# A new hand-written order, wider weights in one small product, and a last scaling on two engines in a banded-attention and mixture-of-experts kernel

## The chip, the cores and the metric

One Trainium2 chip; the kernel runs on one of its cores. The metric is the device time of one execution in microseconds (us). Times inside an execution come from one profiled execution and count from the start of its span.

## The reference

Attention over a band of 65 tokens (batch 8, 8 heads, 576 tokens, head size 64) is followed by a layer in which each of the 4608 tokens goes to the one expert with the largest biased logit. The bias depends on the token's modality, which is 0 or 1.

```python
mask = np.abs(pos[:, None] - pos[None, :]) <= 32
scores = np.where(mask, (q @ k^T) / 8, -1e9); attn = softmax(scores); x = attn @ v      # x: [4608, 512]
logits = x @ w_gate + modality_bias[modality_id]                                        # 8 experts
e_idx = argmax(logits); gate_w = softmax(logits)[e_idx]
out[mask_e] = gate_w * (relu(x[mask_e] @ w1[e]) @ w2[e])                               # w1: 512x1024, w2: 1024x512
```

The kernel assumes that the bias decides, so that all tokens of a modality go to one expert. It checks this on the chip by flags and has a general path behind a branch, which is not taken with the inputs drawn.

## The kernel before

The program is one straight list of steps. A string, `ORDER`, names the steps, and a loop at its end calls them one after another; each engine then executes its own instructions in that order and waits only on semaphores. Nothing reorders them later. A step such as `U1.2:7` has a name (`U`), numbers (token tile 1, part 2) and the PSUM banks it writes (7); a suffix such as `/a`, `/v`, `/p` picks ScalarE (ACT), VectorE (DVE) or GpSimd (POOL). A step in front of another on the same engine therefore delays it, whatever it waits for.

Attention, per batch element b (8 of them): `l` loads a half of q or k (GpSimd's DMA queue, 288 KB, into a ring of 8 buffers), `lw` and `lv` load v; `t` and `tv` transpose on DVE; `TV` and `vc` finish v for b = 0, 1, 2. `SA`/`SB` are the score products, with `MA`/`MB` adding a band mask for the first three halves; `sa`/`sb` are the exponentials on ACT. `M` multiplies by a 0/1 mask on DVE where `MA`/`MB` were not used; that mask is built by `Ka` and spread by `Kb`, both on POOL. `V` is the product with v, `v` divides by the row sum on DVE.

Sorting by modality: `Kh` clears a buffer (DVE), `Ki` loads the modality ids into it (five DMAs on SP's queue), `Kd`, `Kt0` to `Kt2` and `Kr0` to `Kr2` turn them into places by counting (`lpf`, `offs`). `o` makes a one-hot matrix from `lpf` (five compares on POOL, or one on DVE). `H` multiplies x by it, `a` copies the sorted columns into `xl`; `J` multiplies four numbers per token (`valx`) by it and `j` copies those into `cl`. Modality 0 fills `xl` from the left, modality 1 from the right; tiles 0 to 17 (256 tokens, even numbers from the left) and the extra tile 18 (128 tokens, in the middle, with weights of its own) are made of it.

Experts: `W1.i` and `W2.i` load the weights of modality i (2: the extra tile), each 1 MB in bf16, on GpSimd's queue; the expert's number is read from `sp_i`. `G` and `r` make logits, gate and row number of a tile pair; `U` is the first product (8 matmuls of 256 columns, four parts a tile), `u` the relu, `D` the second product in halves (4 matmuls of 512 columns), `y` scales by the gate weight, and `O` scatters 128 rows to the output by an indirect DMA from POOL. `X` is a pair of matmuls on zeros that fill an otherwise idle TensorE. `N` is a drain of POOL. `Kc6`, `Kf0` and `Kf2` prepare limits and flags on POOL; `Z` steps end in the flag that the last branch reads.

GpSimd's DMAs rotate over eight semaphores; one of them is issued only when the DMA eight before it has landed. PSUM has eight banks, `xl` is shared by all tiles, the results of `y` rotate over six buffers.

Of the kernel before, what the change touches and what calls it, by code (L numbers as in the profile page):

```python
# [43 lines left out]
J0:45 j0.0 j0.1 j0.2 j0.3 j0.4 v3 t1.1.0 tv1.0 MA1.0:0123 X13:6 SA1.0:0123 tv2.0 tv1.1 t2.0.0 t2.0.1 sa1.0 SB1.1:4567
X1:3 TV1.0:012 X8:3 sb1.1 vc1.0/a SA1.1:4567 H0.0:3 H0.1:0 V4:12 sa1.1 TV1.1:567 H0.3:4 v4 H0.2:1 X12:2 H0.4:2 Kb/p
lw2.1 W1.1 l2.1.1 l2.0.1 o2/p a0.0 a0.1 a0.2 a0.3 a0.4 W1.0 M7 vc1.1/v V5:01 l3.0.0 Kg l3.1.0 J1:34 W2.1 l3.1.1 Ky1
V7:56 v5 j1.0 j1.1 j1.2 j1.3 j1.4 l3.0.1 v7 TV2.0:012 U1.2:7 SA2.0:3456 M6 vc2.0/a U1.3:0 V6:12 sa2.0 u1.3/a SB2.0:3456
sb2.0 u1.2/v W2.0 l4.1.0 U1.0:0 tv2.1 v6 H1.0:1 u1.0/a a1.0 t2.1.0 t2.1.1 M9 H1.1:2 U1.1:7 u1.1/v M8 TV2.1:345 H1.2:0
U0.3:6 U0.2:1 u0.3/v vc2.1/a a1.1 a1.2 u0.2/a V9:34 H1.4:2 H1.3:5 G0:0 V8:67 a1.3 a1.4 v9 U0.1:1 SB2.1:2345 r0.5 v8 G1:6
r0.0 r1.0 r0.1 r1.1 t3.0.1 r0.2 u0.1/a sb2.1 U0.0:0 U2.2:1 u0.0/v SA2.1:2345 U2.0:7 U2.3:0 u2.2/a sa2.1 r1.5 r1.2 t3.0.0  # L50
E1 u2.3/a SA3.0:1234 Kc8 lv3.0 l4.0.0 D1.0.0:5 U2.1:0 sa3.0 SB3.0:1234 u2.0/a u2.1/a M11 t3.1.1 r0.7 M10 E0 r0.3 r0.4
t3.1.0 sb3.0 D1.1.0:6 D1.0.1:5 U3.2:0 y1.0/v Ko1 V10:12 D1.1.1:6 V11:34 y1.1/a U3.0:5 U3.3:6 u3.3/a u3.2/v v10 v11
SA3.1:0123 u3.0/v J2:45 sa3.1 j2.0 j2.1 j2.2 D2.0.0:7 U3.1:6 SB3.1:0123 D2.0.1:7 M12 r1.7 r1.3 t4.0.1 r1.4 y2.0/v M13
j2.3 u3.1/a j2.4 D0.1.0:6 H2.1:5 H2.2:4 H2.0:7 D0.1.1:6 sb3.1 V13:12 D2.1.0:0 y0.1/v t4.0.0 v13 H2.3:3 a2.0 a2.1 a2.2
D2.1.1:0 y2.1/a a2.3 M15 SB4.0:4567 V12:12 D0.0.0:0 H2.4:3 sb4.0 D0.0.1:0 v12 M14 lv3.1 V15:12 y0.0/v v15 l4.1.1 r0.6
t4.1.1 SA4.0:4567 l4.0.1 O1.1 a2.4 U4.2:3 u4.2/a U4.0:0 u4.0/a sa4.0 r1.6 l5.1.0 lv4.0 O1.0 o3/p l5.0.0 t4.1.0 U4.3:1
U5.3:0 V14:23 SB4.1:4567 u5.3/v sb4.1 v14 U4.1:0 G2:2 U5.2:3 u5.2/a SA4.1:4567 sa4.1 u4.1/a l5.1.1 lv4.1 u4.3/v r2.5
r2.0 t5.0.1 D3.1.0:1 U5.0:2 H3.1:3 H3.0:5 u5.0/a D3.1.1:1 H3.4:0 H3.2:2 H3.3:4 J3:67 a3.0 a3.1 j3.0 a3.2 D3.0.0:5 M17
y3.1/v M16 t5.0.0 U5.1:1 j3.1 a3.3 V17:23 D3.0.1:5 a3.4 j3.2 y3.0/a j3.3 U7.2:4 u7.2/a j3.4 U7.3:0 u7.3/a u5.1/a r2.1
M18 v17 V16:23 SA5.0:4567 U7.0:0 U7.1:1 l5.0.1 M19 Kc6 O0.1 O2.0 Z1 l6.1.0 o4/p O0.0 v16 t5.1.1 r2.2 V19:23 sa5.0 v19  # L60
SB5.0:4567 u7.1/a u7.0/a sb5.0 D4.0.0:1 D4.1.0:0 V18:23 t5.1.0 E2 v18 SB5.1:4567 D4.0.1:1 G3:2 D5.1.0:3 sb5.1 SA5.1:4567
r2.3 o5/v r2.4 r3.5 r3.0 r3.1 l6.0.0 O3.1 r2.6 O2.1 sa5.1 D4.1.1:0 H4.0:2 D5.1.1:3 a4.0 J4:45 r3.2 r3.7 t6.0.1 y4.0/v E3
j4.0 lv5.0 lv5.1 j4.1 t6.0.0 D7.0.0:1 H4.4:2 D7.0.1:1 H4.2:6 D5.0.0:7 r3.3 r3.4 y5.1/v j4.2 j4.3 j4.4 y4.1/a H4.1:0 a4.1
a4.2 H4.3:3 a4.3 D5.0.1:7 a4.4 U6.1:0 M23 M21 M20 r2.7 M22 y7.0/a y5.0/a V21:45 v21 u6.1/v U6.0:6 V20:23 v20 U8.1:1
D7.1.0:0 SB6.0:2345 sb6.0 u6.0/v u8.1/v D7.1.1:0 V23:67 U9.0:1 G4:5 U8.0:2 V22:34 l6.0.1 v23 o6/v r4.0 t6.1.0 v22 O4.0
o7/p r3.6 l6.1.1 O3.0 O7.0 l7.0.1 O4.1 l7.0.0 l7.1.1 lv6.1 O5.1 U8.2:6 U9.3:7 u9.3/v t6.1.1 u9.0/a u8.0/a y7.1/a
SA6.0:0123 U8.3:4 u8.2/a sa6.0 u8.3/v U9.2:6 SA6.1:0123 H5.0:4 r4.1 t7.1.0 r4.5 u9.2/a U6.2:7 U9.1:6 u9.1/v sa6.1
SB6.1:0123 U6.3:5 t7.0.0 u6.3/v u6.2/a a5.0 H5.2:7 D6.1.0:4 D8.0.0:6 sb6.1 H5.1:0 J5:12 D8.0.1:6 D6.1.1:4 a5.1 a5.2
D6.0.0:0 H5.3:5 D9.0.0:3 D6.0.1:0 H5.4:7 D9.0.1:3 lv6.0 Kf0 M26 r4.2 r4.7 t7.1.1 E4 j5.0 j5.1 j5.2 j5.3 y6.1/a j5.4 a5.3
r4.3 M25 r4.4 M27 V26:12 y8.0/v M24 a5.4 y9.0/a D8.1.0:4 v26 y6.0/a V27:56 SB7.1:0123 v27 U10.2:7 D8.1.1:4 V24:56  # L70
u10.2/v O7.1 l7.1.0 r4.6 O5.0 lv7.0 O9.0 lv7.1 Kf2 O8.0 O6.0 O6.1 U11.3:7 v24 u11.3/v t7.0.1 sb7.1 y8.1/a SA7.1:0123
U11.0:5 U10.0:4 V25:67 sa7.1 SB7.0:0123 u10.0/v v25 u11.0/v sb7.0 U10.1:4 G5:6 U10.3:5 SA7.0:0123 M31 r5.0 u10.1/v sa7.0
U11.2:7 D10.1.0:4 H6.0:0 U11.1:3 u10.3/v r5.1 r5.2 r5.5 a6.0 E5 r5.3 r5.4 H6.2:1 J6:56 H6.4:0 H6.1:2 u11.1/a D11.1.0:3
# [5 lines left out]
D12.1.1:4 D12.0.1:3 Kf3:1 r6.4 r6.7 G7:5 Kf4 U14.1:6 U16.0:7 U17.2:1 u14.1/v u17.2/a U15.2:6 u15.2/a y12.1/v y13.0/v
U15.3:0 G9:6 G8:1 r7.0 r7.5 r8.5 y13.1/a U17.3:2 r7.6 r6.6 r8.6 U15.1:5 r7.1 r8.0 y12.0/v r7.2 r7.7 U14.2:4 U14.0:1  # L80
u14.0/a U17.0:3 u17.0/a U14.3:1 E7 u15.1/a u17.3/a u14.3/a u14.2/a D14.1.0:3 D14.0.0:5 U17.1:1 U15.0:4 D14.0.1:5 r7.3
r8.1 r7.4 r8.2 r8.7 O13.1 O12.0 O12.1 r9.0 r9.1 r9.2 W1.2 U16.1:2 u17.1/a D17.0.0:1 D14.1.1:3 y14.0/a u15.0/a u16.0/a E9
Z0 r9.5 y14.1/a E8 r9.3 r8.3 r8.4 r9.7 r9.4 u16.1/v U16.3:4 D15.0.0:5 D15.1.0:3 D17.1.0:6 D16.0.0:2 D17.1.1:6 O13.0 W2.2
# [1002 lines left out]
```

## Time and profile before

| | us |
|---|---|
| three runs | 226.16, 227.04, 223.16 (median 226.16) |
| profiled execution | 223.96 |
| its span | 222.3 |
| busy: TensorE | 204.5 (92%) |
| busy: DVE | 154.7 (70%) |
| busy: ACT | 141.0 (63%) |
| busy: POOL | 118.7 (53%) |

The profile lists each engine's busy time, how long it waited and which engine or DMA ended each wait. A row of its timeline gives start, duration, engine, line of the code, operation, output and input, the number of instructions in the row, and in brackets the idle time before it with what ended it. PE is TensorE's matmuls, PEld its weight loads, SPq the sync engine's DMA issues, and a q behind an engine its sequencer. In the windows view each engine has its busy time and, in brackets, its number of instructions in the stretch; PEclk is the clock that TensorE was granted, 1.00 being full speed, and the DMA share is that of 16 DMA engines.

### The profile page before, as it was taken

Reading aid. Unit: us, or ns where it says so; the run is one execution under the profiler, and the core shown is the slowest. Engines: PE = TensorE matmul, PEld = TensorE weight load, DVE = VectorE, ACT = ScalarE, POOL = GpSimd, SP = SyncE. Lnnn points to the kernel's source line nnn. Section 1 sums busy time; section 2 is a strip of 40 time slices with the busy share of each in tenths; the row PEclk is TensorE's granted clock in tenths of the full one; section 3 lists DMA queues with packets and bytes.
Section 4 is the critical chain, followed back from the end, with each engine's and each line's share of the span. In section 5 each row is a group of like instructions: output and inputs, shape, how many; then the busy total and the mean of one; then the engine's idle time right before and its main releaser. Section 6 shows DMA issues by size and latency. Waiting matters only on the chain.

```text
span 222.3 us, 6507 instructions
## 1 busy us (share of the span) xinstructions
PE 204.5 (92%) x2669; PEld 145.6 (66%) x2696; DVE 154.7 (70%) x302; ACT 141.0 (63%) x234; POOL 118.7 (53%) x215
## 2 busy tenths in 40 slices
PE   6759888999999999999999999999999999999960
PEld 2436657789666678786577875787488659765620
...
GB/s 68 197 201 131 123 155 207 223 200 212 212 186 205 165 160 196 104 122 138 10 42 154 180 187 193 51 196 4 0 3 143 94 50 3 167 194 204 188 157 55
DMA packets 34055, 30.44 MB, mean 137 GB/s; under 512 B 24889, under 2 KB 24929, under 8 KB 33633
## 3 DMA queue, kind: packets, MB, share of 16 engines
...
q8 instruction: 23, 0.38, 0.7%
q14 instruction: 16, 0.12, 0.2%
q1 hardware_dynamic: 224, 0.05, 0.1%
HBM read 40.96 MB, written 9.70 MB: 228 GB/s over the span
## 4 chain that ended last, share of the span: by engine, by line
PE 76%; DMA 9%; POOL 6%; issue 2%; DVE 2%; SPq 1%; POOLq 0%; DVEq 0%
PE banks L845 28%; PE banks L822 28%; DMA w_sb<-in_moe_w_dram 6%; PE banks L660 6%; PE banks L614 5%; POOL oh L573 3%; PE banks L680 3%; DMA mid<-in_moe_modality_id_dram 2%; PE banks L749 2%; PE banks L711 1%; DVE cl L415 1%; POOL out_dram L866 1%; SPq L285 1%; PE banks L252 1%; POOL qkin L217 1%
## 5 line engine op out<-in xcount | busy, mean ns | idle before, releaser
L866 POOL DMA_INDIRECT out_dram<-ys,ix x37 | 38.9, 1051 | 70.4 <-issue 27.9
L822 PE MATMUL banks<-xl,w_sb 128*128 128x256 bf16 x576 | 70.7, 273 | 0.7 <-DMA w_sb<-in_moe_w_dram 0.7
L845 PE MATMUL banks<-w_sb,hT 128*128 128x512 bf16 x267 | 67.7, 379 | 1.1
L822 PEld LDWEIGHTS <-w_sb 128*128 128x128 bf16 x576 | 53.8, 98 | 11.0 <-issue 1.1
L622 ACT ACTIVATE pt<-banks 128x1536 bf16<-128x1536 f32 x32 | 46.3, 1449 | 18.6 <-PE banks L614 18.4
L837 ACT ACTIVATE hT<-banks 128x512 bf16<-128x512 f32 x45 | 25.8, 599 | 30.0 <-PE banks L822 29.8
L845 PEld LDWEIGHTS <-hT 128*128 128x128 bf16 x296 | 26.6, 98 | 25.5 <-issue 0.5
L582 DVE STREAM_TRANSPOSE qk<-qkin 128x576 int32<-128x576 int32 x32 | 39.0, 1243 | 1.2 <-DMA qkin<-in_q_dram 0.6
L698 ACT CAST xl<-banks 128x704 f32 (+1 forms) x40 | 28.4, 710 | 8.7 <-PE banks L680 8.2
L641 DVE TENSOR_TENSOR pt<-pt,mask 128x1920 bf16<-128x1920 bf16 x26 | 29.8, 1160 | 0.5 <-ACT pt L626 0.3
L671 DVE TENSOR_TENSOR xt<-banks,recs 128x640 bf16<-128x640 f32 x32 | 26.4, 825 | 1.2
L835 DVE TENSOR_SCALAR hT<-banks 128x512 bf16<-128x512 f32 x29 | 19.6, 682 | 9.0 <-PE banks L822 7.9
L660 PEld LDWEIGHTS <-pt 128*128 128x128 bf16 x576 | 21.1, 97 | 2.8 <-DVE pt L641 0.2
L660 PE MATMUL banks<-vt,pt 128*128 128x65 bf16 x576 | 22.6, 193 | 0.0
L573 POOL TENSOR_SCALAR oh<-io_l,lpf 128x128 bf16<-128x128 bf16 x30 | 19.9, 682 | 2.7 <-PE banks L680 1.9
L858 ACT ACTIVATE ys<-banks,gw 128x512 f32<-128x512 f32 x19 | 12.8, 685 | 12.4 <-PE banks L845 9.1
L860 DVE TENSOR_SCALAR ys<-banks,gw 128x512 f32<-128x512 f32 x18 | 13.2, 743 | 10.6 <-PE banks L845 10.5
L614 PE MATMUL banks<-qk 32*128 32x192 bf16 (+1 forms) x640 | 18.9, 240 | 1.4 <-DVE qk L582 1.3
L614 PEld LDWEIGHTS <-qk 32*128 32x128 bf16 x640 | 12.5, 93 | 8.3 <-issue 6.9
L217 POOL DMA_DIRECT2D qkin<-in_k_dram x16 | 10.3, 642 | 12.1 <-DMA w_sb<-in_moe_w_dram 7.8
L680 PEld LDWEIGHTS <-xt 128*128 128x128 bf16 x160 | 11.2, 114 | 4.6 <-issue 0.7
...
## 6 DMA issues: line engine op xcount, KB each, us to landing
...
pt<-in_moe_w_dram POOLq DMA_DIRECT2D x2, 1024.0 KB, 10.3
...
out_dram<-ys,ix POOLq DMA_INDIRECT x37, 4.0
mid<-in_moe_modality_id_dram SPq DMA_DIRECT2D x3, 8.0 KB
```

The costliest lines, as they stand in the source:

```text
L573: gp.tensor_scalar(out=t_[:, m, :], in0=io_l[:], scalar1=lpf[:, NM * b + m:NM * b + m + 1], scalar2=None, op0=ALU.is_equal)
L582: nc.vector.transpose(qk_t[b % 2][:, g, at:at + S].rearrange("p (t r) -> p r t", r=R), Ct["l", b, u, g][:].bitcast(I32).rearrange("p (r j) ...
L614: nc.tensor.matmul(st[:, h, WIN * i_:WIN * i_ + w_], qk[32 * h:32 * h + 32, c_, QK + k0:QK + k0 + P], qk[32 * h:32 * h + 32, c_, q0:q0 + w ...
L622: nc.scalar.activation(pt[:, :, 2 * part:2 * part + 2, 0:WIN], st[:, :, 0:2 * WIN].rearrange("p h (j c) -> p h j c", c=WIN), ACT.Exp, scal ...
L641: by[eng or "v"].tensor_tensor(out=p_ap, in0=p_ap, in1=mask[:], op=ALU.mult)
L660: nc.tensor.matmul(o_ap, pt[:, c1:c1 + P], vt[:, g0 + j, 0:D + 1], start=(m == 0 and i_ == 0), stop=(i_ == len(mine) - 1), skip_group_chec ...
L671: nc.vector.tensor_tensor(out=x_t[b % NX][:, :, P * hp:P * hp + P].rearrange("p m (h d) -> p h m d", h=2), in0=o_v[:, :, :, 0:D], in1=rec. ...
L698: ins = nc.scalar.copy(windows(xl, n_kd, P, NM * b + m), src)
L822: ins = nc.tensor.matmul(ph[:, u_, :], w1[:, kd, 2 * P * (mi // 2) + mi % 2:2 * P * (mi // 2 + 1):2], xl[:, kd, c0:c0 + n_], start=(kd == ...
L837: nc.scalar.activation(o_ap, i_ap, ACT.Relu)
L845: nc.tensor.matmul(Ct["D", t_, s_], Ct["h", t_][:, kf, P * s_:P * s_ + P], w2[:, kf, :], start=(kf == 0), stop=(kf == n_kf - 1))
L866: ins = nc.gpsimd.indirect_dma_start(out=out, out_offset=bass.IndirectOffsetOnAxis(ap=ix[:, k_, n_:n_ + 1], axis=0), in_=Ct["y", t_, s_][: ...
```

## The change

All of `ORDER` is written anew: the same steps with other places, other banks and in part other engines. `J` gets wider weights. `y` already had a form that splits the columns between ACT and DVE (`/b`); the last tile uses it now.

- `Kh`, which clears the id buffer, stands directly behind `Kw` on DVE. Before, the clearing of `cl` and eight small clears stood ahead of it. Two clears that DVE had move to ACT (`Kp1`), two that ACT had move to DVE (`Kq0`, `Kq1`).
- On POOL, `Kc6`, `Kf0` and `Kf2` move from the middle of the program to its first part; `Ka` and `Kb` stand behind them. `Kc5` moves behind `W1.0`.
- All eight `o` run on POOL (six before), 48 relus on ACT and 26 on DVE (45 and 29 before).
- `W1.2` and `W2.2` stand behind `O11.1`, with 15 scatters after them, instead of around `O13.0`, with 10 and 9. `N` stands behind `O13.1`, with 11 scatters after it (16 before).
- `J` reads 128 neighbouring columns of the packed numbers as its weights instead of the 4 it needs, so it writes 128 partitions of PSUM; the copies read the first 4. The last columns run over the 160 numbers, so the buffer `valw` has 124 more, cleared once in `Kc7`.

```diff
-Km l0.1.0 Kw Kc7 Kj l0.0.0 lw0.0 Kn0 Ke Kh Kx Kq0/a t0.0.1 t0.0.0 X4:7 X3:2 X0:4 X2:3 MB0.0:4567 Ky0 Kp1/v Kv2/v X9:2
+Km l0.0.0 Kw Kh Ki Kv3/v Kq1/v Kq0/v Kc7 l0.1.0 Kv1/v Ke t0.0.0 t0.0.1 Kj lw0.0 Kn0 l0.1.1 X3:3 X11:6 X5:0 X9:6
...
-O16.0 D16.1.1:0 O18.0 Z5 y16.1/a O16.1
+y18.0/v D16.1.0:0 O17.1 Z4:7 Z5 D16.1.1:0 y16.1/b O18.0 O16.1
...
         elif i == 7:
             nc.vector.memset(cl[:], 0.0)
+            nc.vector.memset(valw[:, 4 * NJ:], 0.0)
...
-    valx = const.tile([P, NJ, 4], BF16)
+    valw = const.tile([P, 4 * NJ + P - 4], BF16, name="valw")
+    valx = valw[:, 0:4 * NJ].rearrange("p (n c) -> p n c", c=4)
...
             if m < 4:
-                o_ap = bank([P, 4, P])[0:4, m, :]
+                o_ap = bank([P, 4, P])[:, m, :]
             else:
-                o_ap = bank([P, 4, P], i=1)[0:4, 0, :]
-            nc.tensor.matmul(o_ap[:, 0:width(m)], valx[:, NM * b + m, :], Ct["o", b][:, m, 0:width(m)], start=(m % 4 == 0), stop=True,
+                o_ap = bank([P, 4, P], i=1)[:, 0, :]
+            at = 4 * (NM * b + m)
+            nc.tensor.matmul(o_ap[:, 0:width(m)], valw[:, at:at + P], Ct["o", b][:, m, 0:width(m)], start=(m % 4 == 0), stop=True,
                              skip_group_check=True)
-            Ct["J", b, m] = o_ap
+            Ct["J", b, m] = o_ap[0:4]
```

DVE at the start of the program, before (`mid` is the id buffer of `Kh`, L415 clears `cl`, L438 to L442 are `Kx`, the transposes `t0.0`):

```order
L303 MEMSET zero_b 128x256
L304 MEMSET one_f 128x1
L415 MEMSET cl 128x2368
L424 MEMSET e_119 128x1 x8
L290 MEMSET mid_103 40x256
L437 TENSOR_REDUCE pm<-mb_bc 128x2
L438 TENSOR_TENSOR pe<-mb_bc,pm 128x16
L440 TENSOR_TENSOR pe<-pe,e_119 128x16
L441 TENSOR_REDUCE ext_e<-pe 128x2
L442 TENSOR_SCALAR sp_i<-ext_e 128x2
L582 STREAM_TRANSPOSE qk_77<-qkin_69 128x18x32
L582 STREAM_TRANSPOSE qk_77<-qkin_70 128x18x32
```

The same place after the change (`xl`, `qk` are the clears `Kv3`, `Kq1`, `Kq0`, `Kv1`):

```order
L290 MEMSET mid_103 40x256
L234 MEMSET xl 128x64 x2
L324 MEMSET qk_78 128x2x32
L324 MEMSET qk_78 128x2x64 x2
L324 MEMSET qk_77 128x2x32
L324 MEMSET qk_77 128x2x64 x2
L415 MEMSET cl 128x2368
L416 MEMSET valw 128x62
L234 MEMSET xl 128x64 x2
L425 MEMSET e_119 128x1 x8
L584 STREAM_TRANSPOSE qk_77<-qkin_69 128x18x32
L584 STREAM_TRANSPOSE qk_77<-qkin_70 128x18x32
```

The clear of `mid` moved ahead of the clear of `cl`, and the work on the bias moved behind the first two transposes.

POOL from the mask copy to the second weight load, before (`mask` is `Kb`, `w_sb` are `W1.1` and `W1.0`, `oh` is `o`):

```order
L268 COPY mask<-mask 128x1536
L268 COPY mask<-mask 128x128
L228 DMA qkin_76<-in_v_dram 128x1152
L153 TENSOR_LOAD sp_i
L795 ISA
L795 DMA w_sb<-in_moe_w_dram 128x4096
L217 DMA qkin_69<-in_k_dram 128x1152
L217 DMA qkin_70<-in_q_dram 128x1152
L573 TENSOR_SCALAR oh_101<-io_l,lpf 128x128 x5
L153 TENSOR_LOAD sp_i
L795 ISA
L795 DMA w_sb<-in_moe_w_dram 128x4096
```

After the change, from the first weight load to the same place (`wg_sb` is `Kg`; `one_r` and `d` are `Kf2`):

```order
L798 DMA w_sb<-in_moe_w_dram 128x4096
L217 DMA qkin_69<-in_q_dram 128x1152
L294 DMA wg_sb<-in_moe_w_gate_dram 128x32
L575 TENSOR_SCALAR oh_100<-io_l,lpf 128x128 x5
L228 DMA qkin_70<-in_v_dram 128x1152
L537 MEMSET one_r 1x128
L538 TENSOR_SCALAR d_774<-ce 1x1
L540 TENSOR_SCALAR d_774<-ce 1x1
L268 COPY mask<-mask 128x1536
L268 COPY mask<-mask 128x128
L153 TENSOR_LOAD sp_i
L798 ISA
```

The mask copy moved from in front of the first weight load to directly in front of the second; `Kf2` moved in ahead of it, and behind `W1.1` POOL goes through one one-hot and the mask.

TensorE at the first `J`, before:

```order
L711 LDWEIGHTS valx
L711 MATMUL banks<-oh_99,valx 4x96
L711 LDWEIGHTS valx
L711 MATMUL banks<-oh_99,valx 4x128
L711 LDWEIGHTS valx
```

After:

```order
L714 LDWEIGHTS valw
L714 MATMUL banks<-oh_99,valw 128x96
L714 LDWEIGHTS valw
L714 MATMUL banks<-oh_99,valw 128x128
L714 LDWEIGHTS valw
```

Each product has 128 output partitions instead of 4; their number and moving columns are the same.

More of the change, by code (lines that the diff above doesn't have):

```diff
@@ L44 @@
[L44 to L73, printed above, removed]
@@ L79 @@
[L79 to L83, printed above, removed]
@@ new lines @@
+Kc0 l1.1.1 Kd t0.1.1 Kp1/a Kp0/a sb0.0 sa0.0 lw1.1 Kc1 Kt0:0 Kr0 t0.1.0 TV0.0:123 vc0.0/a Kr3 lw2.0 l1.0.1 MB0.1:4567
+SB0.1:4567 Kt1:3 X1:0 Kp2/v Ky0 tv0.1 sb0.1 TV0.1:012 Kr1 t1.0.1 vc0.1/a Kt2:3 MA0.1:4567 SA0.1:4567 X6:0 sa0.1 Kr2
+t1.0.0 V0:23 V1:01 t1.1.1 v0 v1 Ko0 MB1.0:4567 SB1.0:4567 o0/p Kc6 l2.0.0 lw1.0 l2.1.0 sb1.0 V3:23 v3 V2:01 J0:23 v2
+j0.0 j0.1 j0.2 j0.3 j0.4 MA1.0:4567 SA1.0:4567 t1.1.0 tv1.1 tv1.0 sa1.0 X12:0 SB1.1:0123 X8:7 tv2.0 t2.0.1 sb1.1 X4:4
+TV1.0:567 vc1.0/a SA1.1:1234 X0:0 V4:56 l2.1.1 t2.0.0 Ka Kf0 W1.1 l2.0.1 Kg o1/p lw2.1 Kf2 Kb/p W1.0 l3.0.0 Ky1 l3.1.0
@@ new lines @@
+Kc5 H0.0:0 H0.1:7 v4 sa1.1 a0.0 a0.1 H0.2:1 a0.2 TV1.1:234 H0.3:0 X13:5 V5:67 H0.4:5 M7 a0.3 a0.4 vc1.1/v J1:01 v5 V7:23
+W2.1 o2/p l3.0.1 v7 M6 j1.0 j1.1 j1.2 j1.3 j1.4 l3.1.1 TV2.0:456 U1.2:7 vc2.0/a SA2.0:0123 V6:45 U1.3:6 sa2.0 u1.3/a
+u1.2/v t2.1.0 v6 tv2.1 SB2.0:0123 sb2.0 U1.0:7 H1.0:4 G0:5 U1.1:6 TV2.1:012 t2.1.1 W2.0 l4.0.0 M9 r0.0 r0.1 r0.5 u1.0/v
+M8 a1.0 l4.1.0 lv3.0 lv3.1 l4.1.1 u1.1/a vc2.1/a H1.2:3 H1.1:4 U0.1:6 a1.1 a1.2 H1.4:5 V9:01 U0.3:2 H1.3:3 u0.3/a a1.3
+a1.4 U0.2:4 u0.1/v v9 V8:67 SB2.1:0123 v8 sb2.1 t3.0.1 t3.0.0 U2.0:5 U2.3:6 u2.3/a U0.0:7 u0.0/a SA2.1:0123 sa2.1 u2.0/a
```

47 lines of the change are left out of this document (36 added, 11 removed).

## The prediction

> **What bounds the kernel now.** I read the windows first, to see where TensorE is full.
>
> ```profile
> 20.00:40.00 20.00, 17.20 (x335) 13.05 (x336) 18.95 (x27) 17.13 (x28) 17.19 (x30) 1.00 0.85 151
> 40.00:50.00 10.00, 9.32 (x146) 7.99 (x144) 9.27 (x12) 8.74 (x13) 3.74 (x9) 1.00 1.08 212
> 50.00:200.00 150.00, 148.94 (x1960) 108.17 (x1978) 107.62 (x212) 99.31 (x171) 71.11 (x104) 1.00 0.77 125
> 214.80:222.30 7.50, 0.00 (x0) 0.00 (x0) 0.00 (x0) 0.68 (x1) 1.45 (x2) 0.80 0.21 69
> ```
>
> The numbers behind the stretch's length are TensorE, its weight loads, DVE, ACT and POOL, then the granted clock, the DMA share and GB/s. From 50 to 200 us TensorE is busy 148.94 of 150 us at full clock, and no other engine is above 72%. A new order can gain there only by making a product itself cheaper; it can lose there. What it can win otherwise lies in front of 50 us and in the 7.5 us behind the last product. From 20 to 40 us DVE is busy 18.95 of 20, so that stretch is DVE's, with the waits that feed it. The timeline shows them:
>
> ```profile
> 1.77 2.03 DVE L415 MEMSET cl<- 128x2368 uint32 x1 [0.44 <-issue]
> 4.20 0.76 SPq L283 DMA_DIRECT2D mid<-in_moe_modality_id_dram  x1
> 12.43 0.22 DVE L467 CAST midr<-mid 40x128 bf16<-40x128 int32 x1 [2.03 <-DMA mid<-in_moe_modality_id_dram]
> 13.87 2.27 DVE L582 STREAM_TRANSPOSE qk<-qkin 128x576 int32<-128x576 int32 x2
> 19.57 2.97 POOL L573 TENSOR_SCALAR oh<-io_l,lpf 128x128 bf16<-128x128 bf16 x5 [0.69 <-DVE lpf L496]
> 27.62 1.71 POOL L268 COPY mask<-mask 128x1536 bf16<-128x1536 bf16 x2
> 29.81 0.53 POOL L795 DMA_DIRECT2D w_sb<-in_moe_w_dram  x1
> 34.29 0.57 POOL L795 DMA_DIRECT2D w_sb<-in_moe_w_dram  x1
> 35.66 1.15 DVE L641 TENSOR_TENSOR pt<-pt,mask 128x1920 bf16<-128x1920 bf16 x1
> 36.72 1.35 DVE L268 CAST vt<-banks 128x1152 bf16<-128x1152 f32 x1
> 38.44 0.72 PE L660 MATMUL banks<-vt,pt 128*128 128x65 bf16 x18
> 39.20 1.28 PE L252 MATMUL banks<-ident,xl 128*128 128x64 bf16 x20
> 40.76 1.05 PE L822 MATMUL banks<-xl,w_sb 128*128 128x256 bf16 x8 [0.28 <-DMA w_sb<-in_moe_w_dram]
> 48.42 1.92 PE L822 MATMUL banks<-xl,w_sb 128*128 128x256 bf16 x16 [0.38 <-DMA w_sb<-in_moe_w_dram]
> ```
>
> DVE stood 2.03 us for the modality ids, and the transposes behind it stood too. POOL then waited 0.69 us for `lpf`, from 18.88. The way to the first expert product is M7 (35.66), vc1.1 (36.72), V7 (38.44), TV2.0 (39.20) and U1.2 (40.76), and the second weight is just late at 48.42.
>
> **The head, step by step.** The clear of the id buffer stood behind the clear of `cl` (1.77 to 3.80), and the request went out at 4.20. Now the clear of the id buffer has that place, so I estimate the request at about 1.8 and the ids at 12.43 - 2.4 = 10.0. They are then no longer waited for: DVE has three transposes ahead of the cast. Up to `lpf` it has six transposes of 2.27/2 = 1.14 us and some ten small operations of about 0.22 (the cast's row), 9.0 us in all; begun about 6 us into the program, and with a load or two to wait for, that gives `lpf` at 16 to 17. On POOL, `Ka` and `Kc5` no longer stand ahead of the first one-hot, and one load more does. These rows price them, and what now stands between that one-hot and the mask copy:
>
> ```profile
> 14.97 0.28 POOL L338 MEMSET mask<- 128x192 bf16 x1
> 16.03 0.15 POOL L347 MEMSET mask<- 128x64 bf16 x1
> 17.51 0.78 POOL L401 TENSOR_SCALAR wf<-iof 128x1 f32<-128x1 f32 x4
> 79.01 0.19 POOL L330 IOTA ioi<- 128x8 int32 x1
> 79.26 1.15 POOL L331 CAST iof<-ioi 128x8 f32<-128x8 int32 x1
> 80.77 0.11 POOL L413 MEMSET lim<- 1x24 f32 x1
> 127.16 0.14 POOL L511 MEMSET fl<- 128x8 f32 x1
> 129.19 0.19 POOL L526 TENSOR_TENSOR fr<-ce,lo__2719 1x8 f32<-1x8 f32 x1
> 12.25 0.22 POOL L331 CAST iof<-ioi 128x40 f32<-128x40 int32 x1
> 79.22 1.15 DVE L641 TENSOR_TENSOR pt<-pt,mask 128x1920 bf16<-128x1920 bf16 x1
> L573 POOL TENSOR_SCALAR oh<-io_l,lpf x30: 590/604/1468, 19.6 to 116.4; 128x128 bf16<-128x128 bf16 x30
> ```
>
> `Ka` took 14.97 to 16.18 (1.21) and `Kc5` 17.51 to 18.88, where POOL came free (1.37); a load costs its issue, about 0.55, as the weights' rows have it. POOL is free at 18.88 - 1.21 - 1.37 + 0.55 = 16.85, which is also where `lpf` comes; I let the one-hot start at 16.8. `Kc6` took 79.01 to 80.88, 1.87, but 0.93 of it is a cast of 8 numbers that took 1.15 us where one of 40 numbers took 0.22. The slow one ran beside DVE's mask product, which starts at 79.22. In the new place no mask product runs before the mask is made, so I take 0.94. The Trainium skill, SBUF — State Buffer, section Who interferes with whom, says that a DVE instruction with two SBUF inputs contends with a GpSimd instruction that reads SBUF; the two rows at 79.2 agree, and by that rule too `Kc6` is the cheap one here.
>
> From 16.8 on POOL: one-hot 2.97, `Kc6` 0.94, four loads 2.2, `Ka` 1.21, `Kf0` 2.22 (127.16 to 129.38), W1.1 0.53 and an estimated 0.3 for reading the expert's number, which no row shows, a load and `Kg` 1.1, one-hot 2.97, load 0.55, `Kf2` 0.56 (three operations at the mean of `Kf0`'s twelve, 0.19), mask copy 1.71. That is 17.3 us without a wait, and the mask is ready at 34.1. W1.1 goes out near 26.6 instead of 29.81. DVE, rid of the 2.03 us and part of the waits behind it, would be at M7 near 33, so **the mask is now what M7 waits for**, 34.1 instead of 35.66: 1.5 us gained. Behind it DVE needs 1.06 and 1.35 (36.5), V7 and what surrounds it 0.76 (38.44 to 39.20) and TV2.0 1.28 (to 38.5). W1.1 lands by 26.6 + 10.95 = 37.6, if it takes as long as before (29.81 to 40.76). U1.2 gains up to 2.2; I take 2.0, since small waits will recur. Behind U1.2 TensorE is dense in both orders. Bounds: -0.6 (the mask at 36.3, by the dear cast and a wait of the length of the 0.69 above) and +3.4 (M7 when DVE alone is ready, and W1.1 in time for it).
>
> **J.** The chain of waits tiles TensorE's time without overlap:
>
> ```profile
> 72.85 0.62 PE banks L680 x12
> 109.33 0.34 PE banks L711 x5
> 109.68 0.97 PE banks L845 x4
> 111.90 0.86 PE banks L845 x4
> L711 PEld LDWEIGHTS <-valx x40: 80/84/85, 26.8 to 169.5; 128*4 128x4 bf16 x40
> L680 PEld LDWEIGHTS <-xt 128*128 128x128 bf16 x160 | 11.2, 114 | 4.6 <-issue 0.7
> ```
>
> J takes 0.34 us and the D half behind it 0.97 instead of 0.86: 0.45 together. H streams the same one-hot with 128 output columns, 12 matmuls in 0.62, so five are 0.26. The wide J should run as H does and save 0.19 each. J0 and J1 lie in the head; J2 to J7 save 6 x 0.19 = 1.15 us. The other bound is a loss: a load of weights is 114 ns against 84, and if that stood free, 30 of them would cost 0.9. I take the gain, because H hides the same loads under its matmuls. The Trainium skill, TensorEngine Tiling (Array Packing), section Key Properties, says that changing the tiling mode drains TensorE; by that rule, the trace agrees, the 0.11 behind J goes with the 4-column form.
>
> **The tail.**
>
> ```profile
> L913 POOLq DRAIN  x1: 4165/4165/4165, 168.4 to 168.4; - x1
> L1081 POOLq DRAIN  x3: 52/103/1539, 219.9 to 222.0; - x3
> 214.30 0.98 POOL L866 DMA_INDIRECT out_dram<-ys,ix  x1 [0.30 <-DVE t_i L906]
> 214.79 0.69 ACT L858 ACTIVATE ys<-banks,gw 128x512 f32<-128x512 f32 x1 [2.06 <-PE banks L845]
> 215.75 0.98 POOL L866 DMA_INDIRECT out_dram<-ys,ix  x1 [0.48 <-ACT ys L858]
> ```
>
> The last scaling of 0.69 us on two engines is about 0.4, but a scatter takes 0.98 and had 0.30 ahead of it, so the last one moves from 215.75 to 214.30 + 1.28 = 215.6: 0.15 gained. The closing drain of 1.54 us has 11 scatters since the last drain instead of 16 and two weight loads: 0.1 gained, between 0 and 0.5. `N` itself, 4.17 us, now stands behind `O13.1` and r9.6, which are through when y12.0 and six small DVE operations are, with 26 pieces of 0.86 still to come on TensorE: about 23 us ahead of its end. The next scatter needs y12.1, some 16 us ahead of that end, so the drain is covered by about 3 us, and the 11 scatters, 14.1 us, fit behind it. W1.2 and W2.2 go out earlier: nothing in the rows waited for them, so nothing is gained. Three relus more on ACT, busy 99.31 of 150 us, cost nothing.
>
> Sum: 2.0 + 1.15 + 0.25 = 3.4 us. The profiled execution took 223.96 (its span 222.3 and 1.66 around it), so its like would take 220.6. The four executions shown (223.16, 223.96, 226.16, 227.04) have a mean of 225.1, 1.1 below the median of the three runs and 1.1 above the profiled one; I put the next median there too: 225.1 - 3.4 = **221.7 us**.
>
> **Rivals.** *The second weight becomes the wait.* W1.0 goes out behind the mask at 34.3, as before, and was in use from 48.42. If it takes 14.1 us again, TensorE, which gets there 2 us sooner, waits for it and keeps 0.4 of the head: 225.1 - 0.4 - 1.4 = 223.3. For it: 212 GB/s from 40 to 50 us, the DMA engines full. Against: 151 GB/s from 20 to 40, and W1.1 and its loads go 3 us sooner, so less is queued. *Slower: POOL late with the mask.* The one-hot's row has 1468 ns beside 604. If the second one-hot ran at that price, 5 x 0.87 = 4.3 us, the mask would come at 38.4 and M7 2.7 later than before: 225.1 + 2.7 - 1.4 = 226.4. From a mask at 37.1 on it outweighs the other gains. Against: the slow cast had a mask product beside it, and here none can run yet. *Better: the mask in time.* M7 at 33: 225.1 - 2.7 - 1.4, less small waits, 220.7. *The drain uncovered.* If POOL comes to `N` 7 us late, four of them fall to the end and the sum turns: 225.6. *A stall in the dense stretch* that no row here announces, from another bank or buffer being reused too soon: 1 us or so at each of a few places, 224 to 230.
>
> **How the numbers follow.** Chances: forecast 0.45, second weight 0.18, POOL late 0.12, mask in time 0.10, drain 0.05, stall 0.10. Medians scatter by about 1.9 us either way, as the three runs do. The range reaches from 219.2 (mask in time, a low draw) to 226.4 (POOL late, a middle draw). A measurement here tells 2% (4.5 us) from no change. Faster by that is below 221.6, which half of the forecast's draws reach, a fifth of the second weight's and most of the mask's: 0.36. Slower, above 230.7, needs a stall, or POOL late with the drain, and a high draw: 0.06. Within 2%: 0.58.
>
> **What would show it.** Right: the id cast without a wait on its DMA; the first one-hot near 17 us; M7 waiting for POOL near 34; U1.2 near 38.7; J as one row of about 0.26 us and no dearer D half behind it; the drain beginning near 190 us, and no late scatter. Wrong: a wait of TensorE for `w_sb` near 46 us, M7 past 37 us, or idle TensorE behind 50 us.

## The result, and the profile after

The kernel after takes 222.53 us (median of 15 runs, 221.46 to 223.79), the kernel before 224.45 us (15 runs, 223.15 to 227.04). The ratio is 0.9924 with a 95% interval of 0.9900 to 0.9948: 1.7 us faster, between 1.2 and 2.2. The ratio is that of the fast runs; the medians alone differ by 1.9 us. The forecast was 221.7 us, a gain of 3.4. The direction is right and the time is 0.8 us off, but about half of the gain is missing.

| | before, us | after, us |
|---|---|---|
| profiled span | 222.3 | 220.5 |
| first expert product U1.2 starts | 40.76 | 39.18 |
| TensorE's last product ends | 214.75 | 213.39 |
| last scatter is issued | 215.75 | 214.74 |
| from there to the end of the span | 6.55 | 5.76 |

The windows of the kernel after have the same columns as those of before.

```profile
20.00:40.00 20.00, 16.03 (x301) 12.27 (x297) 16.94 (x24) 14.86 (x26) 17.25 (x55) 1.00 1.06 193
40.00:50.00 10.00, 9.97 (x184) 8.90 (x182) 9.88 (x16) 8.86 (x13) 8.65 (x13) 1.00 1.06 203
50.00:200.00 150.00, 148.48 (x1940) 106.64 (x1938) 104.11 (x206) 100.55 (x172) 72.21 (x95) 1.00 0.76 127
213.00:220.50 7.50, 0.39 (x2) 0.00 (x0) 0.48 (x1) 0.47 (x1) 1.94 (x2) 0.67 0.24 83
```

From 20 to 40 us DVE is now busy 16.94 of 20 us instead of 18.95, and the stretch from 40 to 50 us is full for TensorE (9.97 of 10). From 50 to 200 us TensorE stands 1.52 us (150 - 148.48), and the two waits shown further down, 0.36 and 1.15 us, are all of it. The 1.06 us of before was no waiting: behind 48.42 us that trace has no gap of TensorE over 0.06 us, and 22 of the 296 matmuls of `D` are missing from it. The timeline of the head shows what DVE, POOL and TensorE wait for:

```profile
1.61 0.76 SPq L283 DMA_DIRECT2D mid<-in_moe_modality_id_dram  x1
10.42 0.21 DVE L469 CAST midr<-mid 40x128 bf16<-40x128 int32 x1
16.93 2.98 POOL L575 TENSOR_SCALAR oh<-io_l,lpf 128x128 bf16<-128x128 bf16 x5
20.07 0.19 POOL L331 CAST iof<-ioi 128x8 f32<-128x8 int32 x1
27.33 0.61 POOL L798 DMA_DIRECT2D w_sb<-in_moe_w_dram  x1 [0.94 <-issue]
33.34 1.70 POOL L268 COPY mask<-mask 128x1536 bf16<-128x1536 bf16 x2
35.07 1.16 DVE L643 TENSOR_TENSOR pt<-pt,mask 128x1920 bf16<-128x1920 bf16 x1 [1.51 <-ACT xl L700]
37.55 0.71 PE L662 MATMUL banks<-vt,pt 128*128 128x65 bf16 x18 [1.21 <-DVE vt L268]
39.18 1.06 PE L825 MATMUL banks<-xl,w_sb 128*128 128x256 bf16 x8
```

The id cast no longer waits. M7 starts at 35.07, right behind the mask copy (33.34 + 1.70 = 35.04), after DVE has stood 1.51 us; the releaser named is ACT, but the copy is what ended last. One trace fixes these times only roughly: in the six other traces with the same head, or with `J` alone changed in it, the first one-hot starts between 16.82 and 18.13 us and U1.2 between 39.10 and 40.35, and in each of them M7 starts within 0.04 us of the end of the mask copy. No expert product waits for its weights. Further on two waits of TensorE are new:

```profile
94.59 0.71 PE L662 MATMUL banks<-vt,pt 128*128 128x65 bf16 x18 [0.36 <-DVE xt L673]
182.05 1.10 POOL L869 DMA_INDIRECT out_dram<-ys,ix  x1 [6.32 <-issue]
183.45 0.99 POOL L869 DMA_INDIRECT out_dram<-ys,ix  x1 [0.30 <-issue]
188.71 0.75 DVE L863 TENSOR_SCALAR ys<-banks,gw 128x512 f32<-128x512 f32 x1 [7.22 <-DMA out_dram<-ys,ix]
189.38 0.15 DVE L773 TENSOR_TENSOR lo<-banks,bias 128x8 f32<-128x8 f32 x1
189.59 1.02 PE L848 MATMUL banks<-w_sb,hT 128*128 128x512 bf16 x4 [1.15 <-DVE lo L773]
```

The last five rows are one chain. The scatters at 182.05 and 183.45 are O13.0 and O10.0, in that order on POOL's queue. The result of y10.0 had long been there, but O13.0 ahead of it had to wait for y13.0. The scaling at 188.71 is y12.0, which writes the buffer that O10.0 sends off (six buffers take turns), so DVE stood 7.22 us until that scatter had landed. r9.0 stands behind y12.0 on DVE and frees the PSUM bank that D15.0.0 writes, and so TensorE stood 1.15 us. The end:

```profile
212.35 1.04 PE L848 MATMUL banks<-w_sb,hT 128*128 128x512 bf16 x4
213.47 0.47 ACT L861 ACTIVATE ys<-banks,gw 128x256 f32<-128x256 f32 x1 [2.15 <-PE banks L848]
213.98 0.48 DVE L863 TENSOR_SCALAR ys<-banks,gw 128x256 f32<-128x256 f32 x1 [1.38 <-ACT ys L861]
214.74 0.97 POOL L869 DMA_INDIRECT out_dram<-ys,ix  x1 [0.69 <-DVE ys L863]
L916 POOLq DRAIN  x1: 3252/3252/3252, 190.4 to 190.4; - x1
L1084 POOLq DRAIN  x3: 46/103/950, 218.7 to 220.2; - x3
```

The two halves of the last scaling run one after the other: DVE begins when ACT has ended, and both together take 0.99 us where ACT alone took 0.69 before. The closing drain takes 0.95 us instead of 1.54.

The 1.8 us of the span add up so: 1.6 from the head, about 1.2 from J (six times 0.20, below), less 1.15 at D15.0.0 and 0.36 at V16, plus 0.1 that no single row accounts for, make 1.36 at TensorE's end. Behind that the last scatter comes 0.35 later than before, counted from TensorE's end (1.35 us instead of 1.00), and from it to the end 0.79 is saved, 0.59 of it in the closing drain. The wait at V16 is in every trace of the new order (0.36 to 1.14 us), and no experiment took it out.

### The profile page after: what moved, and what is told of

Read it like the earlier page. It is cut to its first block, busy times and chain, and to the rows that moved or that the text cites. A ratio compares the mean times of both kernels' runs of the same rounds, so it can differ in the third digit from the quotient of the medians.

```text
span 220.5 us, 6570 instructions
## 1 busy us (share of the span) xinstructions
PE 204.6 (93%) x2696; PEld 144.8 (66%) x2696; DVE 151.5 (69%) x303; ACT 143.8 (65%) x233; POOL 124.0 (56%) x225
## 4 chain that ended last, share of the span: by engine, by line
PE 75%; DMA 8%; POOL 6%; issue 5%; DVE 3%; ACT 1%; POOLq 0%; DVEq 0%; ACTq 0%
PE banks L848 27%; PE banks L825 26%; PE banks L662 7%; PE banks L616 6%; DMA qkin<-in_v_dram 5%; PE banks L682 4%; DMA out_dram<-ys,ix 2%; PE banks L252 2%; PE banks L752 2%; POOL oh L575 1%; POOL qkin L217 1%; PE banks L714 1%; DVE xl L239 1%; ACT pt L624 1%; DVE vt L268 1%
## 5 line engine op out<-in xcount | busy, mean ns | idle before, releaser
L825 PE MATMUL banks<-xl,w_sb 128*128 128x256 bf16 x576 | 71.8, 273 | 0.0
L848 PE MATMUL banks<-w_sb,hT 128*128 128x512 bf16 x288 | 70.7, 379 | 1.2 <-DVE lo L773 1.2
L840 ACT ACTIVATE hT<-banks 128x512 bf16<-128x512 f32 x48 | 27.6, 598 | 21.4 <-PE banks L825 17.7
L863 DVE TENSOR_SCALAR ys<-banks,gw 128x512 f32<-128x512 f32 (+1 forms) x19 | 13.9, 731 | 24.0 <-PE banks L848 14.6
L838 DVE TENSOR_SCALAR hT<-banks 128x512 bf16<-128x512 f32 x26 | 17.9, 687 | 13.1 <-PE banks L825 7.0
L575 POOL TENSOR_SCALAR oh<-io_l,lpf 128x128 bf16<-128x128 bf16 x40 | 26.4, 679 | 0.2
L861 ACT ACTIVATE ys<-banks,gw 128x512 f32<-128x512 f32 (+1 forms) x19 | 12.8, 675 | 17.0 <-PE banks L848 16.5
L722 ACT CAST cl<-banks 4x176 f32 (+1 forms) x40 | 11.4, 285 | 5.4 <-PE banks L714 4.4
L672 DVE RECIPROCAL recs<-banks 128x10 f32<-128x10 f32 x32 | 6.7, 208 | 11.8 <-PE banks L662 9.8
L682 PE MATMUL banks<-oh,xt 128*128 128x128 bf16 (+1 forms) x160 | 13.6, 215 | 0.2 <-ACT pt L624 0.2
```

Of the source, the lines that this page charges most:

```text
L575: gp.tensor_scalar(out=t_[:, m, :], in0=io_l[:], scalar1=lpf[:, NM * b + m:NM * b + m + 1], scalar2=None, op0=ALU.is_equal)
L825: ins = nc.tensor.matmul(ph[:, u_, :], w1[:, kd, 2 * P * (mi // 2) + mi % 2:2 * P * (mi // 2 + 1):2], xl[:, kd, c0:c0 + n_], start=(kd == ...
L840: nc.scalar.activation(o_ap, i_ap, ACT.Relu)
L848: nc.tensor.matmul(Ct["D", t_, s_], Ct["h", t_][:, kf, P * s_:P * s_ + P], w2[:, kf, :], start=(kf == 0), stop=(kf == n_kf - 1))
```

## The experiments

They ran in three groups, each on another chip and with its own runs of the kernel before. It took 230.23, 229.09 and 229.15 us in them, 2 to 2.6% more than in the runs above (the last section shows what the traces have of this), so times are compared inside a group or as ratios to the kernel before.

| group | kernel | median, us | ratio to before (95%) |
|---|---|---|---|
| 1 | after, O10.0 first | 226.84 | 0.9858 (0.9824 to 0.9892) |
| 1 | after, Kf0 and Kf2 late | 226.99 | 0.9877 (0.9830 to 0.9924) |
| 1 | before, wide J | 229.37 | 0.9971 (0.9943 to 0.9999) |
| 1 | after, narrow J | 228.61 | 0.9940 (0.9913 to 0.9967) |
| 2 | after | 227.25 | 0.9933 (0.9902 to 0.9963) |
| 2 | after, all three mends | 226.24 | 0.9895 (0.9864 to 0.9926) |
| 2 | after, N early | 233.16 | 1.0197 (1.0156 to 1.0238) |
| 2 | before, Kh and Ki early | 227.93 | 0.9964 (0.9936 to 0.9991) |
| 3 | after | 226.93 | 0.9903 (0.9865 to 0.9942) |
| 3 | after, O10.0 first, y16.1 on ACT | 226.22 | 0.9880 (0.9839 to 0.9921) |
| 3 | after, all three mends | 225.57 | 0.9828 (0.9781 to 0.9876) |
| 3 | after, Kh and Ki late | 228.01 | 0.9967 (0.9935 to 0.9999) |

**The kernel after, unchanged.** It went along in the second and third group.

> The kernel after, unchanged, as the measure for the three others of this group. If its gain over the kernel before does not hang on the chip: ratio 0.992 again (0.990 to 0.995), with the 1.2-us wait of TensorE at D15.0.0 and the last scaling in two steps as in its first trace.

> The kernel after, unchanged, as the measure for the others of this group: ratio to the kernel before 0.992 to 0.994, as in the two groups before.

Its gain is the same there (0.9933 and 0.9903 beside 0.9924), and the wait at D15.0.0 is there again, in this row of the second group's trace:

```profile
193.90 0.75 DVE L863 TENSOR_SCALAR ys<-banks,gw 128x512 f32<-128x512 f32 x1 [7.15 <-DMA out_dram<-ys,ix]
194.78 1.02 PE L848 MATMUL banks<-w_sb,hT 128*128 128x512 bf16 x4 [1.09 <-DVE lo L773]
```

**The late scatter.** The theory is that D15.0.0 waits because O10.0 stands behind O13.0.

```diff
-... u15.0/a O10.1 O11.1 W1.2 W2.2 r6.6 Z6 O13.0 ... u15.3/a O10.0 r7.6
+... u15.0/a O10.0 O10.1 O11.1 W1.2 W2.2 r6.6 Z6 O13.0 ... u15.3/a r7.6
```

> The kernel after, with O10.0 issued ahead of O10.1 instead of behind O13.0. In the kernel after, y12.0 waited until 188.7 us for the buffer that O10.0 had still to send off, r9.0 stood behind it on VectorE, and TensorE waited 1.15 us at D15.0.0 for r9.0 to free its bank. Theory (late scatter): with O10.0 gone out about 13 us sooner, neither y12.0 nor D15.0.0 waits, and the time falls by 1.15 us, from 222.5 to 221.4 (ratio to the kernel before 0.987). Rival (the chain is late anyway): y12.0 or D15.0.0 waits just as long for something else, such as gate weights or another buffer, and the time stays at 222.5 (0.992).

The timeline of this kernel has O10.0 at 172.48, and y12.0 at 191.72 waits for nothing but its own product:

```profile
172.48 0.97 POOL L869 DMA_INDIRECT out_dram<-ys,ix  x1 [7.99 <-issue]
191.72 0.75 DVE L863 TENSOR_SCALAR ys<-banks,gw 128x512 f32<-128x512 f32 x1 [3.49 <-PE banks L848]
```

The wait of TensorE at D15.0.0 is gone here, as in the two other kernels that have O10.0 first; every kernel of the order after without that edit has it. Laid beside the second group's kernel after, step by step, TensorE is 1.47 us behind it ahead of D15.0.0 (a later head) and 0.22 us behind it afterwards, so the wait is worth 1.25 us and is not given back. The time agrees with the 0.987 expected, 0.9858, though the group did not hold the kernel after itself. Another edit, made for the drain, moved the same scatter the other way:

```diff
-... O10.1 O11.1 W1.2 W2.2 ... y15.1/a r9.6 N O12.1
+... O10.1 N O11.1 W1.2 W2.2 ... y15.1/a r9.6 O12.1
```

> The kernel after with N between O10.1 and O11.1, so that 16 scatters and two weight loads follow it, as in the kernel before. Theory (the closing drain grows with what was issued since the last one): it takes 1.5 us instead of 0.95 and the time is 0.6 us longer than the kernel after (ratio to the kernel before 0.995). Rival (the closing drain varies by itself): 0.9 to 1.0 us, and no longer than the kernel after, unless scatters that stand behind the early drain come late for the buffers of y.

These rows of the kernel with N early are O10.0, y12.0 and D15.0.0, and the closing drain:

```profile
189.88 0.99 POOL L869 DMA_INDIRECT out_dram<-ys,ix  x1 [0.30 <-issue]
197.87 0.75 DVE L863 TENSOR_SCALAR ys<-banks,gw 128x512 f32<-128x512 f32 x1 [9.96 <-DMA out_dram<-ys,ix]
198.75 1.86 PE L848 MATMUL banks<-w_sb,hT 128*128 128x512 bf16 x4 [3.90 <-DVE lo L773]
L1084 POOLq DRAIN  x3: 46/103/1534, 229.4 to 231.5; - x3
```

The closing drain came as the theory put it, 1.53 us, and late scatters came on top: it is the slowest of all, 1.0197, 5.9 us above the kernel after of its group. The drain took 3.86 us in the middle of POOL's queue and moved the scatters and the two weight loads behind it closer together; the buffer of O10.0 was not in use again before 8.0 us after its issue (189.88 to 197.87; 5.2 in the kernel after), and TensorE stood 3.90 us at D15.0.0. Of the 5.9 us, 1.2 had come up by then in the head and in the waits that differ from trace to trace, and 2.8 are the longer stand at D15.0.0. Behind it 1.4 more are lost, because the granted clock fell: from 198 to 201 us it was 0.52, and the four matmuls of D15.0.0 took 1.86 us instead of 1.02. The last 0.6 are the drain.

**The mask in the head.** `Kf0` and `Kf2` went back to the middle of the program:

```diff
-... Ka Kf0 W1.1 l2.0.1 Kg o1/p lw2.1 Kf2 Kb/p W1.0 ... lv7.1 o7/p ... O9.1 D11.1.1:4
+... Ka W1.1 l2.0.1 Kg o1/p lw2.1 Kb/p W1.0 ... lv7.1 o7/p Kf0 ... O9.1 Kf2 D11.1.1:4
```

> The kernel after, with Kf0 (2.2 us on POOL) and Kf2 (0.7 us) put back into the middle of the program, behind the last one-hot and behind O9.1. Theory (the mask is what the head waits for): M7, which waited for the mask until 35.04 us, finds it at about 32.1 us and starts when VectorE is free, at 33.6; U1.2 moves from 39.2 to about 37.8 us, and the time falls by 1.4 us to 221.1 (ratio to the kernel before 0.985). Rival (the weights are next): W1.1 or W1.0 is not there, TensorE waits for w_sb between 38 and 48 us, and the time stays within 0.5 us of 222.5. Second rival (POOL in the middle): the moved steps delay scatters and one-hots near 130 us, and what is won in the head is lost there.

The mask copy, M7, U1.2 and a later row of DVE in this kernel:

```profile
30.03 1.70 POOL L268 COPY mask<-mask 128x1536 bf16<-128x1536 bf16 x2
32.82 1.17 DVE L643 TENSOR_TENSOR pt<-pt,mask 128x1920 bf16<-128x1920 bf16 x1
37.16 1.06 PE L825 MATMUL banks<-xl,w_sb 128*128 128x256 bf16 x8
150.88 0.16 DVE L784 TENSOR_SCALAR ixf<-banks 128x4 f32<-128x4 f32 x1 [5.22 <-remote]
```

M7 starts without a wait at 32.82 and U1.2 at 37.16, where the kernel after had 39.67 and 39.10 in the other groups: the mask was the bound, and no weight is late. But the ratio, 0.9877, is only about 0.4% below that of the kernel after, 0.9 us of the 2.2 won, and the intervals overlap. TensorE was 2.2 us ahead of the second group's kernel after at 145 us, and 0.6 us ahead from 155 us on. In between DVE stood 5.22 us before r5.5. It stood so in all three traces with these steps in the middle, until something that the trace calls "remote"; what that was stays open. It does not explain the loss: every other trace of the new order from these groups has a stand of DVE there too, of 2.5 to 3.8 us, and TensorE stood longer between 145 and 155 us in the second group's kernel after (2.0 us) than here (1.75). What the three traces alone have is the clock. These are two windows of this kernel, with the columns of the windows above, then two rows of TensorE, the second from the second window:

```profile
148.00:151.00 3.00, 1.31 (x21) 0.78 (x19) 0.12 (x2) 1.79 (x4) 1.66 (x2) 0.97 0.59 227
151.00:154.00 3.00, 3.00 (x23) 2.10 (x17) 2.96 (x6) 2.64 (x3) 0.19 (x1) 0.50 0.10 31
143.00 1.92 PE L825 MATMUL banks<-xl,w_sb 128*128 128x256 bf16 x16
151.54 3.21 PE L825 MATMUL banks<-xl,w_sb 128*128 128x256 bf16 x16
```

TensorE was busy for less than half of three microseconds, and then worked at a granted clock of 0.50: the 16 matmuls of U at 151.54 took 3.21 us, where 16 such matmuls took 1.92 us at 143.00. Over the five microseconds from 150 to 155 the clock was 0.66, so 1.7 us of clock were lost (an estimate: 0.34 x 5), which is the size of the 1.6 us given back. The two traces with all three mends (below) have a clock of 0.50 from 151.0 and from 152.4 us on; in all other traces it stays at 1.00 between 45 and 195 us. So the second rival was right that the gain is lost in the middle, but not by late scatters. No run tests what makes the clock fall here.

**The ids.** Two runs take the id request alone, in either direction:

```diff
-before: Km l0.1.0 Kw Kc7 Kj l0.0.0 lw0.0 Kn0 Ke Kh Kx ... X6:3 Ki MA0.0:0123
+before: Km l0.1.0 Kw Kh Ki Kc7 Kj l0.0.0 lw0.0 Kn0 Ke Kx ... X6:3 MA0.0:0123
-after:  Km l0.0.0 Kw Kh Ki Kv3/v Kq1/v Kq0/v Kc7 l0.1.0
+after:  Km l0.0.0 Kw Kv3/v Kq1/v Kq0/v Kc7 Kh Ki l0.1.0
```

> The kernel before with Kh and Ki alone put to the front, Kh behind Kw on VectorE and Ki as soon as it is done. Theory (the id wait alone is worth little, since W1.1 is issued by POOL behind two one-hots and the mask copy and takes 11 us): VectorE no longer waits 2.0 us for the ids, the first one-hot starts 0.7 us sooner and W1.1 goes out 0.7 us sooner, U1.2 starts at 40.0 instead of 40.8 and the time falls by 0.7 us (ratio 0.997). Rival (VectorE alone sets the head): U1.2 moves by the 2.0 us of the id wait, ratio 0.991.

> The kernel after with Kh and Ki behind the clear of cl, where the ids are requested at about 4.9 us instead of 1.6. Theory (the mask, and with it M7, hangs on the ids through lpf and the first one-hot): the ids come at about 13 us, VectorE waits 2.7 us, the first one-hot starts at 19.6 instead of 16.9, the mask is ready 2.7 us later and U1.2 starts near 42; the time grows by 2.7 us, ratio to the kernel before 1.004. Rival (VectorE and POOL have other work to put there): at most 0.5 us longer than the kernel after, 0.995.

W1.1 and the first expert weights in the kernel before with the ids early, then the id cast, the first one-hot and U1.2 in the kernel after with the ids late:

```profile
29.14 0.53 POOL L795 DMA_DIRECT2D w_sb<-in_moe_w_dram  x1
39.57 0.77 PEld L822 LDWEIGHTS <-w_sb 128*128 128x128 bf16 x8 [0.20 <-DMA w_sb<-in_moe_w_dram]
```

```profile
12.68 0.22 DVE L469 CAST midr<-mid 40x128 bf16<-40x128 int32 x1 [2.10 <-DMA mid<-in_moe_modality_id_dram]
17.61 2.94 POOL L575 TENSOR_SCALAR oh<-io_l,lpf 128x128 bf16<-128x128 bf16 x5 [0.75 <-DVE lpf L498]
39.83 1.06 PE L825 MATMUL banks<-xl,w_sb 128*128 128x256 bf16 x8
```

In the first, W1.1 goes out 0.67 us sooner (29.14 instead of 29.81), the weights' load still waits for it, and the ratio is 0.9964 where 0.997 was put. U1.2 starts at 39.58, which is 1.2 us sooner than in the trace of the kernel before (40.76) and not the 0.8 expected; one trace of each cannot tell these apart. In the second, the trace speaks against the theory: DVE waits 2.10 us for the ids, yet the one-hot starts at 17.61 and not at 19.6, and U1.2 at 39.83 and not near 42. Both lie inside the spread of the traces with the ids early (16.82 to 18.13 and 39.10 to 40.35), so the late ids cannot be seen there: DVE has other work in the meantime. The time is 1.1 us longer than that of the kernel after in its group (228.01 beside 226.93), more than the rival's 0.5 and less than the theory's 2.7; where that lies, the trace does not show. So the ids alone bring U1.2 forward in the old order about as far as the whole new head does (39.58 beside 39.10 to 40.35), and in the new order, where the mask is the bound, their place hardly shows in the head.

**J alone.** The wide weights went into the kernel before, and the 4 columns into the kernel after (the six lines of the diff that change `J`, taken alone or back):

```diff
-            nc.tensor.matmul(o_ap[:, 0:width(m)], valx[:, NM * b + m, :], Ct["o", b][:, m, 0:width(m)], ...
+            nc.tensor.matmul(o_ap[:, 0:width(m)], valw[:, at:at + P], Ct["o", b][:, m, 0:width(m)], ...
```

> The kernel before, with the wide weights of J alone: 128 neighbouring columns instead of 4, and the clear of the added columns. Theory (a product with 4 columns is dear): each of the six J behind 60 us and the product behind it lose 0.19 us together, and the time falls by 1.1 us from 224.45 to 223.3 (ratio 0.995). Rival (the weight loads stand free, or the time goes into the next product): between no change and 0.9 us longer (ratio 1.000 to 1.004).

> The kernel after, with J as it was: 4 columns of weights, no added clear. Theory (a product with 4 columns is dear): 1.1 us longer than the kernel after, 223.6 (ratio to the kernel before 0.997). Rival (the width of J is worth nothing): as the kernel after, 222.5 (0.992).

The chain of waits at J4 and J5, first of the kernel before with wide J, then the rows of the kernel before that answer to J5's:

```profile
109.36 0.25 PE banks L714 x5
109.61 0.86 PE banks L848 x4
...
135.26 0.25 PE banks L714 x5
135.51 2.59 PE banks L848 x12
```

```profile
133.81 0.34 PE banks L711 x5
134.16 2.70 PE banks L845 x12
```

Where the kernel before had 0.34 and 0.97 at J4, there are 0.25 and 0.86: 0.20 us. At J5 0.34 and 2.70 (three D halves) became 0.25 and 2.59, 0.20 again. The kernel after has 0.25 too, at 108.93 us. The ratio, 0.9971 (0.9943 to 0.9999), is a gain of 0.7 us, between 0 and 1.3, and holds the 1.1 expected. The way back is no proof by its time: 0.9940 with narrow J lies 0.1 and 0.4% above the kernel after of the other groups, less than the intervals. The rows decide here, not the times.

**Together.** O10.0 first and y16.1 on ACT alone (`y16.1/b` made `y16.1/a`), without and with the move of Kf0 and Kf2:

> The kernel after with O10.0 ahead of O10.1 and y16.1 on ScalarE alone; Kf0 and Kf2 stay where the kernel after has them. Theory (two losses that lie behind the head and are not given back): 1.15 us at D15.0.0 and 0.3 us at the last scaling, 1.45 us or 0.65% less than the kernel after, ratio to the kernel before about 0.986. Rival (what is freed at D15.0.0 goes into the next wait): 0.3 us alone, 0.992.

> The kernel after with O10.0 ahead of O10.1, Kf0 and Kf2 back in the middle of the program, and y16.1 on ScalarE alone. Theory (three separate losses): 1.15 us at D15.0.0, 1.4 us at M7 and 0.3 us at the last scaling, 2.8 us in all: ratio to the kernel before 0.980. Rival (the head's gain is given back): TensorE reaches U1.2 two us sooner, but waits behind it for ScalarE and VectorE, which have the same work to do, and only the other two remain: 0.986.

> The same with Kf0 and Kf2 in the middle as well, a second time. Theory (the head's gain is real but is given back at r5.5 near 147 us, where VectorE stood 5.1 us in both kernels that had these steps in the middle): no faster than the kernel with the other two changes alone, 0.986 to 0.989. Rival (the stand at r5.5 belongs to the chip of those runs): 0.980, and no such wait in the trace.

The last scaling and the last scatter with all three mends, in the second group:

```profile
215.62 1.04 PE L848 MATMUL banks<-w_sb,hT 128*128 128x512 bf16 x4
216.75 0.69 ACT L861 ACTIVATE ys<-banks,gw 128x512 f32<-128x512 f32 x1 [2.15 <-PE banks L848]
217.71 0.97 POOL L869 DMA_INDIRECT out_dram<-ys,ix  x1 [0.39 <-issue]
```

From the end of TensorE (215.62 + 1.04) to the last scatter it is 1.05 us, where the kernel after has 1.35: the 0.3 expected. The two mends alone gave 0.9880 where 0.986 or, by the rival, 0.992 was put: 0.7 us below the kernel after of the group, which does not decide between the two. In the trace the stand at D15.0.0 is gone, and its 1.2 us are not given back. All three mends gave 0.9895 and 0.9828. The first is above both what the theory (0.980) and the rival (0.986) had, the second lies between what it was put at (0.986 to 0.989) and its rival (0.980). In both groups the kernel with all three is below the kernel after, by 1.0 and 1.4 us of the medians; the intervals of the two overlap in each group. It is faster than the kernel before beyond doubt, and probably faster than the kernel after, by about half of the 2.8 us that the three losses add up to. The stand at r5.5 (5.1 us) was there both times, so it does not belong to the runs of one group. In the third group TensorE was 1.3 us ahead of the kernel with two mends from U1.2 on and 0.02 us behind it at 160 us, after the stretch at the clock of 0.50. Not every execution need lose that: of the six of this kernel, the three with a mean granted clock of 0.990 or more took 224.10 to 225.23 us, the three with 0.984 or less 225.91 to 226.73.

## Why the prediction was right and wrong

- **What bounds the kernel:** right. TensorE stayed full behind the head (148.48 of 150 us), and the gains lie in the head, in J and at the end.
- **The ids and the first one-hot:** right. The request went out at 1.61 (put at 1.8), the cast did not wait, the one-hot started at 16.93 (put at 16.8). That this needed the early ids was not shown: with them late it started at 17.61, inside the spread of the traces with them early.
- **POOL's list up to the mask:** right in kind, 0.9 us short. `Kc6` took 0.85 (19.87 to 20.72; put at 0.94), with the cast of 8 numbers at 0.19 instead of 1.15 us. The Trainium skill, SBUF — State Buffer, section Who interferes with whom, says that a DVE instruction with two SBUF inputs contends with a GpSimd instruction that reads SBUF; the trace agrees, DVE had none beside this cast, but a transpose with one input. `Kf0` took 2.21 (put at 2.22). The term that was too small is the reading of the expert's number, 0.94 us of wait in front of W1.1 instead of the estimated 0.3; `Kf2` took 0.83 instead of 0.56, and the one-hot started 0.13 later, so the mask came at 35.04 instead of 34.1. The reading is not always a wait: in front of W1.0, behind the 1.70 us of the mask copy, none shows (34.98). That the mask is what M7 waits for was right, and the kernel with Kf0 and Kf2 late shows it.
- **U1.2:** 1.6 us gained instead of 2.0 (39.18). M7 gained only 0.6, but behind it V7 no longer started 0.37 us late (J1, which stood ahead of it on TensorE, was through by then), the 0.28 for the weight went away, since W1.1 was issued 2.5 us sooner, and about 0.35 came from smaller pieces up to U1.2. The difference between 1.6 and 2.0 is within the spread of the traces (39.10 to 40.35). The rival of the second weight fell: nothing waited for `w_sb`. One bound does not come out of its own terms: 34.1 with the dear cast (0.93 more) and a wait of 0.69 is a mask at 35.7, not 36.3. Nor does the rival "the mask in time": 225.1 - 2.7 - 1.4 is 221.0, not 220.7.
- **J:** right, in size too: 0.20 us (put at 0.19) at both places where the two traces were laid side by side.
- **The tail:** wrong in both terms, in opposite directions, so that their sum, 0.44 us gained instead of 0.25, was near by luck. The last scaling was put at 0.4 us on two engines; it took 0.99, since DVE waits for ACT's half. The program orders the two: the DVE instruction waits for ACT's. The prediction left that wait out. That they are ordered because both write one buffer is likely, but no run tested it. The closing drain was put at 0.1 us of gain, between 0 and 0.5; it was 0.59.
- **N:** covered, as put. It began at 190.4 and no scatter was late behind it.
- **"Behind U1.2 TensorE is dense in both orders":** the step that failed. The list of steps was walked for POOL's head, the drain and the weights, but not for the six buffers of `y`: which scatter each scaling needs, and what stands ahead of that scatter on POOL. It cost 1.15 us at D15.0.0, about what J gained, and V16 cost 0.36 more: these 1.5 us, put at nothing, are nearly all that the gain fell short by. A stall of this kind stood among the rivals, with a chance of 0.10 and without a place, and idle TensorE behind 50 us stood among the signs of being wrong. "W1.2 and W2.2 go out earlier, so nothing is gained" may also have been too kind: they stand ahead of O13.0 and O10.0, and O10.0 landed 5.2 us after its issue, where the median of the scatters is 3.3. With 3.3, y12.0 would have begun 1.9 us sooner, and D15.0.0 would not have waited (an estimate); that the loads slowed it was not tested by itself.
- **The number:** in part luck. The kernel before was put at 225.1 us and measured 224.45, so 0.65 us of the missing gain does not show in the time of 222.53 beside 221.7.
